# Keys, queries and values handed over with the dimensions in rows

## The chip, the core and the metric

The kernel runs on one core of a Trainium2 chip. Its time is device microseconds of the whole program. The engines named here: TensorE (PE; its weight loads are PEld), VectorE (DVE), ScalarE (ACT), GpSimd (POOL) and SyncE (SP), which issues nearly all transfers. Inputs lie in the chip's memory, and the form in which they lie there is chosen ahead of the launch, outside the time.

## The reference

```python
def _attn_ref(q, k, v):                     # B, H, S, D = 2, 8, 768, 64
    block, window = (32, 16)
    k_sum = k.reshape(B, H, nb, block, D).max(axis=3)
    v_sum = v.reshape(B, H, nb, block, D).mean(axis=3)
    scores_l = scale * np.matmul(q, k.transpose(0, 1, 3, 2))
    mask_l = np.abs(pos[:, None] - pos[None, :]) < window
    scores_s = scale * np.einsum('bhsd,bhnd->bhsn', q, k_sum) + np.log(block)
    scores_l_m = np.where(mask_l, scores_l, -1000000000.0)
    a = softmax of [scores_l_m, scores_s]   # written out in the reference
    return np.matmul(a, np.concatenate([v, v_sum], axis=2))

def _moe_ref(x, w_gate, w_val, w_out):      # 1536 tokens, 512 -> 1536 -> 512
    g = x @ w_gate
    return (g * sigmoid(g) * (x @ w_val)) @ w_out

def _moe2_ref(x, w_in, w_out):              # 512 -> 2048 -> 512
    h = x @ w_in
    return (h * np.clip(h + 3.0, 0.0, 6.0) / 6.0) @ w_out
```

Each query sees the 31 keys within 15 positions, and 24 summaries of blocks of 32 keys (the maximum of the keys, the mean of the values). The output goes through two MLPs. The weights are handed over in 8-byte floats.

## The kernel before, in words

**Tiles.** 1536 rows are cut into four token tiles of T = 384: t = 0, 1 are batch 0, t = 2, 3 batch 1. The 8 heads go in NP = 4 pairs c, whose 2 x 64 dimensions fill 128 partitions. A stage of attention is one t with its four pairs.

**Attention of one pair.** `keys` (once for each batch) loads k with the positions in rows, two parts of 384 positions, each by two transfers of 64 dimensions; TensorE turns each part by three transposes (`rows`, line 592), ScalarE or VectorE copies the bank into `kT[c]`, and VectorE takes the maxima over blocks into `ksum[c]` (line 621). `queries` does the same for 384 queries and multiplies by -1/8 on the way out. `values` (once for each batch) loads v with eight neighbouring positions in one of 96 partitions, adds halves three times on GpSimd or VectorE (line 636), and TensorE multiplies by a small matrix of 1/32 (line 642), which gives the 24 means; they are copied six times over into the first 24 rows of `vw[c]`. `load_vw` fills rows 24 to 119 of `vw[c]` with the 96 positions that each of six blocks of 64 queries can see. `scores` writes 120 columns for each of 384 queries (line 697); VectorE adds a mask and takes the top (717), ScalarE the exponentials (724), VectorE sums and reciprocals (736, 737), GpSimd or VectorE weighs (748), TensorE turns the weights (754), and `outputs` multiplies with `vw` (768). The result becomes x in two parts, a high and a rest (lines 273, 280).

**MLP.** Every product is three matmuls (lines 334 to 336): high by high, low by high, high by low. The weights come as 8-byte floats and are split on VectorE and ScalarE (lines 370 to 391, then 273 and 280), group by group; the first group is loaded and split while attention runs, the next ones behind it, into room that attention gives back.

**What sets the order.** `Plan` collects tasks with a rank, costs on each engine and what they read and write, schedules them once by those costs and emits the instructions of all engines in that order. Each engine then runs its list in order; semaphores make it wait. Transfers stand in SyncE's list too (those of pair 1 of t=0 in ScalarE's), so one that waits for its buffer holds back all behind it. Where TensorE's plan has a gap, `fill` puts up to ten matmuls on zeros there (line 835). Attention of t=1 to 3 is spread among the MLP's first group. The ranks are shifted by the table `LEAD`.

## Time and profile before

| what | us |
|---|---|
| median of 3 runs | 653.56 |
| lowest and highest | 653.07, 653.57 |
| profiled execution | 654.63 |
| its span, first to last instruction | 652.9 |
| TensorE busy | 640.2 (98%) |
| VectorE busy | 438.3 (67%) |
| ScalarE busy | 289.7 (44%) |
| GpSimd busy | 52.9 (8%) |

A busy share is a mean over the whole program: the first fifth, with attention in it, and the rest are two different programs. A matmul's time in the rows overlaps its neighbours', so what one costs is read from start to start. The idle time in brackets is that of the engine just before the row, with what ended it.

### The profile page before, as it was taken

Reading aid. Unit: us, or ns where it says so; the run is one execution under the profiler, and the core shown is the slowest. Engines: PE = TensorE matmul, PEld = TensorE weight load, DVE = VectorE, ACT = ScalarE, POOL = GpSimd, SP = SyncE. Lnnn points to the kernel's source line nnn. Section 1 sums busy time; section 2 is a strip of 40 time slices with the busy share of each in tenths; the row PEclk is TensorE's granted clock in tenths of the full one; section 3 lists DMA queues with packets and bytes.
Section 4 is the critical chain, followed back from the end, with each engine's and each line's share of the span. In section 5 each row is a group of like instructions: output and inputs, shape, how many; then the busy total and the mean of one; then the engine's idle time right before and its main releaser. Section 6 shows DMA issues by size and latency. Waiting matters only on the chain.

```text
span 652.9 us, 11688 instructions
## 1 busy us (share of the span) xinstructions
PE 640.2 (98%) x4576; PEld 601.1 (92%) x4576; DVE 438.3 (67%) x972; ACT 289.7 (44%) x674; POOL 52.9 (8%) x73
## 2 busy tenths in 40 slices
PE   7799999999999999999999999999999999999997
PEld 6688888999999999999999999999999999999996
DVE  3789974589997978369754997286738753333332
ACT  3788788455543433134322564354424332222220
POOL 3435443100000000000000000000000000000000
PEclk9989999999999999999999999999999999999999
DMA  8998944043433233003210133012301000000112
GB/s 185 220 225 232 193 85 140 1 130 132 159 130 98 97 97 97 1 27 103 81 50 0 66 103 124 1 65 64 131 1 40 25 1 0 2 1 0 50 49 96
DMA packets 73319, 53.84 MB, mean 82 GB/s; under 512 B 45744, under 2 KB 66736, under 8 KB 73264
## 3 DMA queue, kind: packets, MB, share of 16 engines
q1 hardware_dynamic: 70864, 52.51, 28.7%
q10 hardware_dynamic: 2400, 0.59, 0.6%
q8 instruction: 36, 0.59, 0.4%
q14 instruction: 19, 0.16, 0.1%
HBM read 49.94 MB, written 3.15 MB: 81 GB/s over the span
## 4 chain that ended last, share of the span: by engine, by line
PE 92%; DMA 4%; ACT 2%; issue 0%; SPq 0%; DVE 0%; POOL 0%; ACTq 0%; POOLq 0%
PE mm L334 16%; PE mm L335 15%; PE mm L336 15%; PE mmb L334 13%; PE mmb L335 13%; PE mmb L336 13%; PE at_s L697 2%; PE pv L768 2%; DMA vn<-in_v 2%; DMA early<-in_k 1%; PE at_t L754 1%; ACT p L724 1%; DMA kn<-in_k 1%; PE pv L835 1%; PE at_q L592 1%
## 5 line engine op out<-in xcount | busy, mean ns | idle before, releaser
L334 PE MATMUL mm<-x,wa 128*128 128x384 f32 x196 | 69.2, 353 | 0.0
L336 PE MATMUL mm<-x,wa 128*128 128x384 f32 x196 | 65.9, 336 | 0.0
L335 PE MATMUL mm<-x,wa 128*128 128x384 f32 x196 | 65.9, 336 | 0.0
L387 ACT ACTIVATE raw<-raw 128x512 f32<-128x512 f32 x68 | 46.2, 680 | 26.3 <-DVE bits L379 23.4
L335 PE MATMUL mmb<-x,wb 128*128 128x384 f32 x160 | 53.5, 335 | 0.0
L335 PE MATMUL mm<-x,wb 128*128 128x384 f32 x160 | 53.5, 335 | 0.0
L336 PE MATMUL mmb<-x,wb 128*128 128x384 f32 x160 | 53.5, 334 | 0.0
L336 PE MATMUL mm<-x,wb 128*128 128x384 f32 x160 | 53.5, 334 | 0.0
L334 PE MATMUL mm<-x,wb 128*128 128x384 f32 x160 | 53.5, 334 | 0.0
L334 PE MATMUL mmb<-x,wb 128*128 128x384 f32 x160 | 53.5, 334 | 0.0
L273 ACT ACTIVATE g<-u 128x384 fp32r<-128x384 f32 x61 | 32.0, 525 | 43.5 <-DVE u L431 22.6
L391 DVE SCALAR_TENSOR_TENSOR bits<-raw,bits 128x512 f32<-128x512 f32 x68 | 46.6, 685 | 1.1 <-ACT raw L387 0.6
L379 DVE SCALAR_TENSOR_TENSOR bits<-raw,bits 128x512 uint32<-128x512 uint32 x68 | 46.9, 690 | 0.4
L383 DVE SCALAR_TENSOR_TENSOR bits<-raw,bits 128x512 uint32<-128x512 uint32 x68 | 46.9, 690 | 0.1
L280 DVE TENSOR_TENSOR g<-u,g 128x384 fp32r<-128x384 f32 x59 | 33.5, 568 | 19.2 <-ACT g L273 19.1
L273 ACT ACTIVATE gb<-u 128x384 fp32r<-128x384 f32 x51 | 26.8, 525 | 37.4 <-DVE u L431 19.2
L724 ACT ACTIVATE p<-p,st 128x120 f32<-128x120 f32 x96 | 36.9, 388 | 10.5 <-DVE st L717 10.5
L335 PE MATMUL mmb<-x,wa 128*128 128x384 f32 x124 | 41.5, 335 | 0.0
L336 PE MATMUL mmb<-x,wa 128*128 128x384 f32 x124 | 41.5, 334 | 0.0
L334 PE MATMUL mmb<-x,wa 128*128 128x384 f32 x124 | 41.5, 334 | 0.0
L273 ACT ACTIVATE wb<-bits 128x512 fp32r<-128x512 f32 x33 | 20.9, 633 | 44.6 <-DVE bits L391 16.9
L280 DVE TENSOR_TENSOR gb<-u,gb 128x384 fp32r<-128x384 f32 x51 | 28.3, 555 | 16.7 <-ACT gb L273 16.6
(198 smaller groups left out, 1659.9 us busy)
## 6 DMA issues: line engine op xcount, KB each, us to landing
raw<-in_moe_w_out SPq DMA_DIRECT2D x28, 512.0 KB, 3.2
raw<-in_moe_w_in SPq DMA_DIRECT2D x16, 512.0 KB, 3.7
raw<-in_moe_w_gate SPq DMA_DIRECT2D x12, 512.0 KB, 4.2
raw<-in_moe_w_val SPq DMA_DIRECT2D x12, 512.0 KB, 3.6
vw<-in_v SPq DMA_DIRECT2D x32, 120.0 KB, 3.6
vn<-in_v SPq DMA_DIRECT2D x8, 384.0 KB, 4.6
out<-oacc SPq DMA_DIRECT2D x11, 256.0 KB, 2.0
kn<-in_k SPq DMA_DIRECT2D x16, 96.0 KB, 4.7
```

Source lines behind the costliest of these rows:

```text
L273: nc.scalar.activation(dst, src, AF.Copy, scale=scale)
L280: eng[e].tensor_tensor(dst, a, b, ALU.subtract)
L334: nc.tensor.matmul(ps, lhsT=lh, rhs=rh, start=j == 0, stop=False)
L335: nc.tensor.matmul(ps, lhsT=ll, rhs=rh, start=False, stop=False)
L336: nc.tensor.matmul(ps, lhsT=lh, rhs=rl, start=False, stop=j == n_k - 1)
L379: nc.vector.scalar_tensor_tensor(t, high_w(), 0xC0000000, t, ALU.bitwise_and, ALU.bitwise_or)
L383: nc.vector.scalar_tensor_tensor(t, low_w(), 29, t, ALU.logical_shift_right, ALU.bitwise_or)
L387: nc.scalar.activation(mag, mag, AF.Abs)
L391: nc.vector.scalar_tensor_tensor(as_f(), mag, 2.0**-15, as_f(), ALU.is_ge, ALU.mult)
L697: nc.tensor.matmul(tiles["at", "s", *names[h]][a * QB : (a + 1) * QB, j, cols], lhsT=q2[hs, u * QB : (u + 1) * QB], rhs=rhs, start=True, s ...
L724: nc.scalar.activation(a, a, AF.Exp, bias=s[:, 0, n : n + 1], scale=-1.0, accum_out=s[:, 1, n : n + 1])
L768: nc.tensor.matmul(tiles[pv][h * D : (h + 1) * D, u * QB : (u + 1) * QB], lhsT=vw[c][:NK, u, h * D : (h + 1) * D], rhs=tiles[pts[h]][:, u ...
```

## The change

The inputs q, k and v are handed over with the dimensions of a head pair in 128 rows and the positions along each row (k with 16 zeros at both ends), and v a second time, as `vu`, with the 64 positions of a block in rows, then the block, then the 128 dimensions, with a block of zeros at both ends. Weights of `w_gate`, `w_val` and `w_in` are handed over so that a partition's 4 KB lie in one piece (four pieces of 1 KB before). So:

- keys: one transfer for a pair, straight into `kT`; no turn, no copy, no memset of its ends. `kT` exists for each batch; three of batch 0 lie in the room of x of t=3.
- queries: one transfer, straight to where scores read them; the factor -1/8 moves into the mask instruction, whose table is scaled to it.
- values: VectorE sums the 768 columns of [128, 768] by blocks of 32 into [128, 24], TensorE transposes this, and the factor 1/32 is applied in the copy to `vw`.
- `vw`: three transfers still, now of 64, 16 and 16 partitions with 3 KB each; its memset is gone.
- costs of transfers in the plan's tasks are lowered to suit; `LEAD` and the other numbers of the plan stay.

```diff
+def laid_out(name, a):
+    if name in ("q", "k", "v"):
+        a = a.reshape(B, NP, 2, S, D).transpose(0, 1, 2, 4, 3).reshape(B, NP, P, S)
+        if name == "k":
+            a = np.pad(a, ((0, 0), (0, 0), (0, 0), (HALO, HALO)))
+    elif name == "vu":
+        a = a.reshape(B, NP, 2, S // QB, QB, D).transpose(0, 1, 4, 3, 2, 5).reshape(B, NP, QB, S // QB, P)
+        a = np.pad(a, ((0, 0), (0, 0), (0, 0), (1, 1), (0, 0)))
+    elif name in ("moe_w_gate", "moe_w_val", "moe2_w_in"):
+        a = a.reshape(KC, P, -1, P).transpose(2, 1, 0, 3)
...
     rings = dict(mm=4, mmb=4, at=3, pv=1, wa=9, wb=9, raw=3, bits=2, u=3, g=5, gb=5,
-                 kn=4, qn=2, v3=1, qT=2, p=4, st=2, pt=4)
+                 v3=1, qT=4, p=4, st=2, pt=4)
...
     def load_vw(t, c):
+        b, half = divmod(t, 2)
+        u0, to = half * NB, vw[c]
+        nc.sync.dma_start(out=to[NS + HALO : NS + HALO + QB], in_=vu[b, c, :, u0 + 1 : u0 + 1 + NB])
+        nc.sync.dma_start(out=to[NS : NS + HALO], in_=vu[b, c, QB - HALO :, u0 : u0 + NB])
+        nc.sync.dma_start(out=to[NS + HALO + QB :], in_=vu[b, c, :HALO, u0 + 2 : u0 + 2 + NB])
...
     def keys(rank, b, c):
+        n = ("kT", b, c)
+        def load():
+            second(2 * b, c).dma_start(out=kT[b, c], in_=k[b, c])
...
-            add(rank, {"pe": 0.3}, turn, r=[n, ("cs",)], w=[ps, ("kT", c)])
-            add(rank - LEAD["k_put"], {"act": 0.4, "dve": 0.47}, put, r=[ps], w=[("kT", c)])
...
-        add(rank, {"dve": 0.87}, most, r=[("kT", c)], w=[("ksum", c)])
+        add(rank - LEAD["k_load"], {"dma": 1.35}, load, w=[n])
+        add(rank, {"dve": 0.87}, most, r=[n], w=[("ksum", c)])
...
+        def total():
+            nc.vector.tensor_reduce(new(v3, [P, NS]), vn[b, c].rearrange("q (n i) -> q n i", i=BLOCK), AX.X, ALU.add)
+        def turn():
+            tiles[ps] = new_bank(ps, [NS, P])
+            nc.tensor.transpose(tiles[ps], tiles[v3], ident)
         def put(e):
-            copy(e, vw[c][:NS], tiles[ps].unsqueeze(1).to_broadcast([NS, NB, P]))
-        add(rank, {"pool": 1.23, "dve": 0.6}, halve(4), w=[room], port=True)
-        add(rank, {"pool": 0.72, "dve": 0.33}, halve(2), w=[room], port=True)
-        add(rank, {"pool": 0.45, "dve": 0.2}, halve(1), r=[room], w=[v3], port=True)
-        add(rank, {"pe": 0.33}, mean, r=[v3, ("masks",)], w=[ps, ("vs", c)])
+            copy(e, vw[c][:NS], tiles[ps].unsqueeze(1).to_broadcast([NS, NB, P]), 1.0 / BLOCK)
+        add(rank, {"dve": 0.87}, total, r=[room], w=[v3])
+        add(rank, {"pe": 0.12}, turn, r=[v3, ("cs",)], w=[ps, ("vs", c)])
...
     def queries(rank, t, c):
-        add(rank, {"pe": 0.3}, turn, r=[n, ("cs",)], w=[ps, qt])
-        add(rank - LEAD["q_put"], {"act": 0.4, "dve": 0.47}, put, r=[ps], w=[qt])
+            second(t, c).dma_start(out=tiles[n], in_=q[b, c, :, half * T : (half + 1) * T])
+        add(rank - LEAD["q_load"], {"dma": 0.68}, load, w=[n])
...
-                scale=1.0, scalar=3.0e38, op0=ALU.add, op1=ALU.min, accum_out=tiles[st][:, 0, h * TR + r : h * TR + r + 1],
+                scale=-SCALE, scalar=3.0e38, op0=ALU.add, op1=ALU.min, accum_out=tiles[st][:, 0, h * TR + r : h * TR + r + 1],
```

The plan is made anew, so the order of all engines moves a little. Three places show it; numbers in the names are t, c and part.

TensorE in stage t=2, around the means of values of pair 0 of batch 1 (`at_v_1_0`), before: `at_q` and `at_k` are turns of queries and keys, `mm_8` an MLP product of x of t=1.

```order
L592 MATMUL at_q_2_1_1301<-cs_89,qn_2_1_1183 128x128 x3
L334 MATMUL mm_8_1310<-x1_1017,wa_0_0_1_0_724 128x384
L335 MATMUL mm_8_1310<-x1_1017,wa_0_0_1_0_724 128x384
L336 MATMUL mm_8_1310<-x1_1017,wa_0_0_1_0_724 128x384
L592 MATMUL at_k_1_2_0_1318<-cs_89,kn_1_2_0_1224 128x128 x3
L642 MATMUL at_v_1_0_1323<-v3_1_0_1273,cs_89 24x128
```

And now:

```order
L351 MATMUL mm_9_1199<-x1_878,wa_0_0_0_1_715 128x384
L352 MATMUL mm_9_1199<-x1_878,wa_0_0_0_1_715 128x384
L353 MATMUL mm_9_1199<-x1_878,wa_0_0_0_1_715 128x384
L351 MATMUL mm_10_1238<-x1_878,wa_0_0_1_1_807 128x384
L352 MATMUL mm_10_1238<-x1_878,wa_0_0_1_1_807 128x384
L353 MATMUL mm_10_1238<-x1_878,wa_0_0_1_1_807 128x384
L615 MATMUL at_v_1_0_1248<-cs_89,v3_1_0_1231 24x128
```

The turns of keys and queries are gone from between the MLP's matmuls, and the product by the matrix of 1/32 is a transpose.

VectorE at the start of the program, before; `vn` are the loaded values, `at_s` the scores, `ksum` the maxima.

```order
L621 TENSOR_REDUCE ksum0_98<-kT0_90 128x24
L636 TENSOR_TENSOR vn0_0_167<-vn0_0_167 96x2x256
L636 TENSOR_TENSOR vn0_1_254<-vn0_1_254 96x2x256
L717 ISA p_0_0_0_226,st_0_0_225<-at_s_0_0_0_218,cs_89 128x120
L717 ISA st_0_0_225 128x1
```

And now; `v3` are the sums of values.

```order
L598 TENSOR_REDUCE ksum0_94<-early_k_98 128x24
L611 TENSOR_REDUCE v3_0_0_198<-vn0_0_152 128x24
L598 TENSOR_REDUCE ksum1_95<-early_k_98 128x24
L611 TENSOR_REDUCE v3_0_1_220<-vn0_1_188 128x24
L676 ISA p_0_0_0_169,st_0_0_168<-at_s_0_0_0_157,cs_89 128x120
L676 ISA st_0_0_168 128x1
```

The sums and the maxima of pairs 0 and 1 now all stand ahead of the first mask add (`p<-at_s,cs`).

SyncE's list at the start, up to the first block of MLP weights (`raw`), before.

```order
L809 DMA cs_89<-in_cst 128x128
L554 DMA early3_107<-in_k 128x3x64 x4
L554 DMA early2_164<-in_q 128x3x64 x2
L575 DMA vn0_0_167<-in_v 96x2x512
L575 DMA vn0_1_254<-in_v 96x2x512
L812 DMA cs_89<-in_cst 128x384
L554 DMA early3_107<-in_k 128x3x64 x4
L554 DMA early2_164<-in_q 128x3x64 x2
L584 DMA vw0_94<-in_v 80x2x64
L588 DMA vw0_94<-in_v 96x5x64 x2
L575 DMA vn0_2_320<-in_v 96x2x512
L554 DMA early3_107<-in_k 128x3x64 x4
```

And now.

```order
L581 DMA vn0_0_152<-in_v 128x768
L581 DMA vn0_1_188<-in_v 128x768
L771 DMA cs_89<-in_cst 128x360
L595 DMA early_k_98<-in_k 128x800
L633 DMA early_q_99<-in_q 128x384
L586 DMA vw0_90<-in_vu 64x768
L587 DMA vw0_90<-in_vu 16x768
L588 DMA vw0_90<-in_vu 16x768
L581 DMA vn0_2_235<-in_v 128x768
L595 DMA kT0_3_100<-in_k 128x800
L633 DMA early_q_99<-in_q 128x384
L586 DMA vw1_91<-in_vu 64x768
```

What stood in four transfers of keys and two of queries stands in one each; the first block of weights comes behind 17 transfers where 29 stood before it.

## Rows read from the trace of the kernel before

**Rows 1.** The page, 40 slices of 16.3 us; each digit a slice, in tenths.
```profile
PE   7799999999999999999999999999999999999997
...
PEclk9989999999999999999999999999999999999999
...
DMA  8998944043433233003210133012301000000112
```

**Rows 2.** Windows: stretch, us, busy us and instructions of each engine, clock, DMA share, GB/s.
```profile
8.40:46.20 37.80, 30.67 (x543) 24.91 (x540) 29.55 (x106) 27.71 (x94) 15.54 (x18) 0.95 1.05 220
...
46.20:67.30 21.10, 20.84 (x314) 18.31 (x316) 19.85 (x69) 18.63 (x64) 10.11 (x12) 1.00 0.88 221
...
10.00:30.00 20.00, 15.96 (x329) 12.62 (x329) 13.69 (x56) 14.61 (x52) 8.28 (x12) 1.00 1.04 212
...
140.00:170.00 30.00, 30.00 (x175) 30.00 (x174) 29.60 (x57) 16.98 (x33) 0.00 (x0) 1.00 0.43 140
...
33.50:37.00 3.50, 3.50 (x24) 2.84 (x20) 3.36 (x8) 3.28 (x8) 1.81 (x2) 0.51 1.18 284
...
66.10:652.90 586.80, 582.48 (x3684) 551.46 (x3680) 389.52 (x801) 241.69 (x517) 24.90 (x29) 1.00 0.22 68
```

**Rows 3.** Timeline of TensorE: start us, us, line, operation, tiles, count, idle before.
```profile
15.39 0.52 PE L592 MATMUL mm_q<-cs,early 128*128 128x128 f32 x3 [1.46 <-DMA early<-in_q]
...
29.52 0.54 PE L754 MATMUL at_t<-cs,p 128*120 128x128 f32 x3 [1.12 <-POOL p L748]
...
31.14 0.34 PE L835 MATMUL at_t<-zeros 128*128 128x128 bf16 x3 [1.08 <-DVE st L717]
...
35.89 0.67 PE L334 MATMUL mm<-x,wa 128*128 128x384 f32 x1
...
60.38 0.49 PE L592 MATMUL at_k<-cs,kn 128*128 128x128 f32 x3
...
60.71 0.49 PE L592 MATMUL at_q<-cs,qn 128*128 128x128 f32 x3
...
65.27 0.92 PE L768 MATMUL pv<-pt,vw 120*64 120x64 f32 x24
...
71.23 0.40 PE L642 MATMUL at_v<-v,cs 96*24 96x128 f32 x2
...
71.56 0.44 PE L334 MATMUL mm<-x,wa 128*128 128x384 f32 x1
...
85.57 0.31 PE L697 MATMUL at_s<-ksum,qT 64*64 64x24 f32 x8
...
86.58 0.44 PE L334 MATMUL mm<-x,wa 128*128 128x384 f32 x1
...
89.88 0.42 PE L334 MATMUL mm<-g,wa 128*128 128x384 f32 x1
```

**Rows 4.** Timeline of VectorE, the same columns.
```profile
8.37 0.95 DVE L621 TENSOR_REDUCE ksum<-kT 128x24 f32<-128x768 f32 x1 [8.37 <-ACT kT L273]
...
18.27 0.28 DVE L717 CUSTOM_DVE_ANT_0 p<-at_s,cs 128x120 f32<-128x120 f32 x1 [2.46 <-PE at_s L697]
```

**Rows 5.** DMA, 0 to 125 us: packets by size; issues, KB each, us to landing.
```profile
DMA packets 51446, 20.88 MB, mean 167 GB/s; under 512 B 44640, under 2 KB 49504, under 8 KB 51424
...
early<-in_k SPq DMA_DIRECT2D x12, 96.0 KB, 3.9
```

**Rows 6.** Timeline of the DMA queue of SyncE: start us, us, line, tiles, count.
```profile
1.18 2.01 SPq L554 DMA_DIRECT2D early<-in_k  x4
...
21.82 0.55 SPq L370 DMA_DIRECT2D raw<-in_moe_w_gate  x1
```

**Rows 7.** Lines of VectorE, 0 to 125 us: busy us, mean ns, idle before.
```profile
L621 DVE TENSOR_REDUCE ksum<-kT 128x24 f32<-128x768 f32 x8 | 7.6, 946 | 8.4 <-ACT kT L273 8.4
...
L636 DVE TENSOR_TENSOR vn<-vn 96x512 f32<-96x512 f32 x5 | 3.9, 803 | 0.5 <-DMA vn<-in_v 0.5
...
L277 DVE COPY kT<-mm_k 128x384 f32<-128x384 f32 x2 | 1.1, 556 | 0.5 <-PE mm_k L592 0.5
```

More of the change, by code (lines that the diff above doesn't have):

```diff
@@ L33 @@
 N1, N2 = F1 // G1, F2 // G2
-WP = 96
 NEG = 1.0e9
+SCALE = 1.0 / D**0.5
 LEAD = dict(
@@ L543, in out2 @@
             add(rank, {"dma": 0.73 * n / DM}, store, r=[("o", t, m)])
-    kT = [ap_.tile([P, S + 2 * HALO], F32, name=f"kT{c}") for c in range(NP)]
-    vw = [ap_.tile([P, NB, P], F32, name=f"vw{c}") for c in range(NP)]
+    vw = [ap_.tile([NK, NB, P], F32, name=f"vw{c}") for c in range(NP)]
     ksum = [ap_.tile([P, NS], F32, name=f"ksum{c}") for c in range(NP)]
     vn = {}
-    def load_rows(dst, src, queue=nc.sync):
-        for h in range(2):
-            queue.dma_start(out=dst[:, :, h * D : (h + 1) * D], in_=src[h].rearrange("(r p) d -> p r d", p=P))
-    early = {}
-    def stage(kind, c, part):
-        x = 3 if kind == "k" else 2
-        if x not in early:
-            early[x] = xpool.tile([P, 8, TR, P], F32, tag=f"x{x}", name=f"early{x}")
-        return early[x][:, 2 * c + part]
+    early_k = xpool.tile([P, NP - 1, S + 2 * HALO], F32, tag="x3", name="early_k")
+    early_q = xpool.tile([P, 2, NP, T], F32, tag="x2", name="early_q")
+    kT = {(b, c): ap_.tile([P, S + 2 * HALO], F32, name=f"kT{b}_{c}") if b or c == NP - 1 else early_k[:, c]
+          for b in range(B) for c in range(NP)}
     def second(t, c):
@@ L573, in load_v @@
         room = xpool.tile([P, KC * T], F32, tag=f"acc{v_room(b, c)}", name=f"vn{b}_{c}")
-        vn[b, c] = room[:WP, : 16 * D].rearrange("p (h r d) -> p h r d", h=2, r=8)
-        nc.sync.dma_start(out=vn[b, c], in_=v[b, 2 * c : 2 * c + 2].rearrange("h (p r) d -> p h r d", r=8))
+        vn[b, c] = room[:, :S]
+        nc.sync.dma_start(out=vn[b, c], in_=v[b, c])
     def load_vw(t, c):
-        b, s0 = divmod(t * T, S)
-        va = v[b, 2 * c]
-        end, cut0, cut1 = (0, HALO, NW) if s0 == 0 else (NB - 1, 0, QB + HALO)
@@ L581, in load_vw @@
-        inner = 1 if s0 == 0 else 0
-        first = s0 + end * QB - HALO + cut0
-        src = bass.AP(va.tensor, va.offset + first * D, [[D, cut1 - cut0], [S * D, 2], [1, D]])
-        nc.sync.dma_start(out=vw[c][NS + cut0 : NS + cut1, end, :].rearrange("p (h d) -> p h d", h=2), in_=src)
-        for h in range(2):
-            first = h * S + s0 + inner * QB - HALO
-            src = bass.AP(va.tensor, va.offset + first * D, [[D, NW], [QB * D, NB - 1], [1, D]])
-            nc.sync.dma_start(out=vw[c][NS : NS + NW, inner : inner + NB - 1, h * D : (h + 1) * D], in_=src)
@@ L590, in rows @@
-    def rows(ps, src):
-        for r in range(TR):
-            nc.tensor.transpose(ps[:, r, :], src[:, r, :], ident)
-    def keys(rank, b, c):
-        for part in range(2):
-            n = ("kn" if b else "k0", b, c, part)
-            def load(n=n, part=part):
-                if b == 0:
-                    tiles[n] = stage("k", c, part)
-                else:
-                    new(n, [P, TR, P])
-                load_rows(tiles[n], k[b, 2 * c : 2 * c + 2, part * T : (part + 1) * T], second(b, c))
-            add(rank - LEAD["k_load"], {"dma": 1.05}, load, w=[n])
-            ps = prep_bank(b, "k", b, c, part)
-            def turn(n=n, ps=ps):
-                tiles[ps] = new_bank(ps, [P, TR, P])
-                rows(tiles[ps], tiles[n])
-            def put(e, part=part, ps=ps):
-                dst = kT[c][:, HALO + part * T : HALO + (part + 1) * T].rearrange("q (r p) -> q r p", p=P)
-                copy(e, dst, tiles[ps])
-            add(rank, {"pe": 0.3}, turn, r=[n, ("cs",)], w=[ps, ("kT", c)])
-            add(rank - LEAD["k_put"], {"act": 0.4, "dve": 0.47}, put, r=[ps], w=[("kT", c)])
+        b, half = divmod(t, 2)
@@ L655, in queries @@
-        b, s0 = divmod(t * T, S)
+        n = ("qT" if t > 1 else "q0", t, c)
+        b, half = divmod(t, 2)
         def load():
             if t < 2:
-                tiles[n] = stage("q", c, t)
+                tiles[n] = early_q[:, t, c]
             else:
-                new(n, [P, TR, P])
-            load_rows(tiles[n], q[b, 2 * c : 2 * c + 2, s0 : s0 + T], second(t, c))
-        add(rank - LEAD["q_load"], {"dma": 1.05}, load, w=[n])
-        def turn():
-            tiles[ps] = new_bank(ps, [P, TR, P])
-            new(qt, [P, TR, P])
-            rows(tiles[ps], tiles[n])
@@ L671, in put @@
-        def put(e):
-            copy(e, tiles[qt], tiles[ps], -1.0 / float(D) ** 0.5)
-        add(rank, {"pe": 0.3}, turn, r=[n, ("cs",)], w=[ps, qt])
-        add(rank - LEAD["q_put"], {"act": 0.4, "dve": 0.47}, put, r=[ps], w=[qt])
+                new(n, [P, T])
+            second(t, c).dma_start(out=tiles[n], in_=q[b, c, :, half * T : (half + 1) * T])
+        add(rank - LEAD["q_load"], {"dma": 0.68}, load, w=[n])
     def scores(rank, t, c):
-        half, qt = t % 2, ("qT", t, c)
+        b, half, qt = t // 2, t % 2, ("qT" if t > 1 else "q0", t, c)
```

53 lines of the change are left out of this document (16 added, 37 removed).

## The prediction

> **What bounds the kernel now.** I read the page's 40 slices first [rows 1]: the reader is to see that TensorE stands at 9 tenths from the third slice on, that its clock sits a little under full in that third slice, and that the DMA row is nearly full only over the first five slices, some 80 us. So there are two regimes, and the change touches only the first. Next the windows [rows 2]: from 66.1 us to the end TensorE is busy 582.48 of 586.8 us, and in 140 to 170 us it is busy all 30 us. Whatever is late after 66 us is late because TensorE has that much to do. Before that it has room: in 8.4 to 46.2 us it is busy 30.67 of 37.80, and part of this is matmuls on zeros. The third view is the timeline of TensorE [rows 3]: the first MLP matmul starts at 35.89 us, and the last output of pair 3 of stage t=1 (the matmuls on vw) starts at 65.27 and takes 0.92, so it ends near 66.1. I call that end T, 66.1 us. The sum has two terms: where T lies, and what TensorE still has to do behind it.
>
> VectorE is the helper that decides T. In 46.2 to 67.3 us it is busy 19.85 of 21.10 (94%) [rows 2]; in the stage before it 29.55 of 37.80, with waits for scores such as 2.46 us ahead of the first mask add of pair 1 [rows 4], scores that in turn stood behind 1.46 us of waiting for that pair's queries [rows 3]. In 10 to 30 us the DMA share is 1.04 at 212 GB/s; in 140 to 170 us a share of 0.43 gives 140, which is 326 GB/s at full share [rows 2]. The packets say why: 44640 of 51446 in the first 125 us are under 512 B [rows 5].
>
> **Term 1, TensorE's work behind T.** A turn of three transposes of keys or queries costs 0.33 us from its start to the next start (60.38 to 60.71) [rows 3]. Behind T the order of before has 5 such turns of keys and 7 of queries; all go: 12 x 0.33 = 4.0 us. The four means of values of batch 1 cost 0.33 each (71.23 to 71.56) and become one transpose, for which I take a third of a turn, 0.11: 4 x 0.22 = 0.9 us. Bounds: 0 (as dear as the mean) and 0.33 (free) each; it is nearest to the turn's row, being the same operation. Two moves run against each other: the order puts the scores of t=2 pair 0 ahead of T, 1.0 us (85.57 to 86.58) [rows 3], and puts 21 MLP matmuls behind T that were ahead of it, at 30 us / 175 = 0.171 each [rows 2], 3.6 us. So 586.8 - 4.0 - 0.9 - 1.0 + 3.6 = 584.5 us.
>
> **Term 2, where T lies.** Stage t=0 first, until the last x of t=0 (46.2 us). VectorE starts there at 8.37 with the maxima of keys [rows 4]. Ahead of them stood four transfers of keys, the first issued at 1.18 [rows 6], two turns and two copies; now it is one transfer on SP, issued at the same place, and the chain of turn and copy is gone. A transfer of 96 KB of early keys takes 3.9 us to land at the median [rows 5]. One four times as large lands between that and 3.9 + 1.4 us (288 KB more at 212 GB/s), so VectorE starts between 5.1 and 6.5. The pieces are long, and the keys and queries of pair 1 now stand at the head of ScalarE's queue and come at the same time; I take 5.5.
>
> Its work in this stage: out go 4 copies of 0.556 and 4 halvings of 0.803, 5.4 us; in come 4 sums of columns, priced by the maxima of keys, the same reduction over the same 128x768, at 0.946 [rows 7], 3.8 us, and one copy of weights, 0.5; the order moves about 2 us of mask adds, reciprocals and weight splitting to the next stage. 29.55 - 5.4 + 3.8 + 0.5 - 2.0 = 26.4 us.
>
> The Trainium skill (VectorE: DVE Perf Modes, "The perf-mode tier table" and "Rules for kernel authors") speaks against this step: a reduction runs only in the slowest mode, and where it lies on the hot path another form is advised. The row agrees: 0.946 us against 0.803 for a halving [rows 7]. By that rule alone VectorE, the busiest helper, gains nothing from the change, which is the second rival below.
>
> Then VectorE's idle time in the stage, 37.80 - 29.55 = 8.25 us [rows 2]. It was waiting for keys and queries that passed through DMA, TensorE and a copy. Twelve turns and their copies go from in front of the scores and transfers come in longer pieces, but the masks still stand behind five transfers on SP, the sums of values of pairs 0 and 1 now stand ahead of the first mask add and wait for their transfers, and ScalarE's exponentials still alternate with VectorE. Bounds 0 and 8.25; I take half, 4.1. The stage ends at 5.5 + 26.4 + 4.1 = 36.0 us.
>
> Stage t=1: VectorE had 19.85 us of work, loses one halving and one copy (1.3), gains one pair of maxima (0.9) and the 2 us moved here: 21.4 us. At the 94% of before that is 22.8, and T lies 1.2 us ahead of its end as before (67.3 less 66.1): 36.0 + 22.8 - 1.2 = 57.6 us. TensorE alone would not be later: its 30 us between 35.89 and T lose 7 turns and 21 matmuls, 2.3 + 3.6, and leave some 24 us of work, of which the first part can run from about 30 us: the first weight block, issued at 21.82 us before, stands behind 17 transfers on SP where 29 stood, at 2.01 / 4 = 0.5 us for issuing one [rows 6], so 6 us earlier. 30 + 24 = 54 us is ahead of 57.6.
>
> What else the change touches, and costs nothing here: ScalarE loses more copies than VectorE and is not ahead of it; the longer pieces of weights come where TensorE has no idle time; GpSimd's halvings and memsets go, and its weighing of exponentials stays. The factor of the scores and the 1/32 of the means ride in instructions that stood there before. Two w_out blocks now stand on SP behind vw loads that wait for outputs of t=1 pairs 0 and 1. Those outputs come before T, and the blocks are first used by matmuls of g on wa, at 89.88 us before [rows 3], some 24 us behind T; that work of TensorE hides the landing and the splitting. Without it the price would be the landing of a transfer, 4 to 6 us.
>
> The Trainium skill (SBUF — State Buffer, "Door 1: The DMA port swizzle") says that a transfer to few partitions reaches few ports. The halos of vw are now two transfers of 16 partitions for each pair and stage, 49 KB each; by its four ports of about 27 GB/s an estimate is 0.45 us each, where the 326 GB/s of the late weights would take 0.15. The eight of t=0 would cost 2.4 us more of DMA time if nothing ran beside them, and by that the prediction would be 645. No row of before shows such a transfer, and the sum doesn't use it.
>
> **Sum.** 57.6 + 584.5 = 642.1 us of span, against 652.9. The profiled execution took 654.63, so 1.7 lies around the span: 643.8, which is 10.8 below it, 1.65%. On the median of 653.56 that is 642.8; I predict 643 us. Its own range is 639 to 647 (idle time of 0 to 8.25 in the first stage).
>
> **Rivals.**
> 1. The forecast: both terms. For it: TensorE is full behind T, so work removed there counts at once. 0.58.
> 2. VectorE takes the gain of the start. Its work to T hardly changes (49.4 before, 47.8 now: the sums take back most of what copies and halvings give). If all its idle time of 8.25 stays and one more wait like the 2.46 of before comes ahead of the first mask add, which now stands behind two sums of values, T = 57.6 + 4.1 + 2.5 = 64.2 and the time is 649.4. For it: 94% busy. Against it: the waits shown there are for turned keys and queries. 0.20.
> 3. TensorE alone bounds from the first MLP matmul on: start at 35.89 less the 6 us of SP and the 2.9 of VectorE's start, 27; 24 us of work; T = 51, 636 us. For it: the order has only 14 fills behind the first MLP matmul. Against it: VectorE would have to do 47.8 us from 5.5 to 52 without a pause. 0.13.
> 4. Slower, by the clock of TensorE. In 33.5 to 37 us the granted clock was 0.51, the 1.2 GHz level, and ahead of it TensorE had waited 1.12 and 1.08 us at 29.5 and 31.1 [rows 2, 3]. The change takes the turns out of a stage in which TensorE is already thin. If the half clock held from the first MLP matmul, 24 us of work would take 48 and T would be 27 + 48 = 75, some 660 us. For the time to pass 653.56 T must pass 69, 42 us for 24 us of work, so it decides from some 36 us of half clock on, ten times what the rows show; in 10 to 30 us, at 15.96 of 20 busy, the clock held, and the order keeps 122 of 132 fills. 0.05.
> 5. No difference: T stays, and the 2.3 us that term 1 takes off are lost to new waits behind T; about 653. 0.04.
>
> Chances, with 0.2% (1.3 us) as what a measurement of this kernel can tell from no change: faster 0.92, same 0.03, slower 0.05. The range goes from rival 3 to rival 2: 635 to 650 us.
>
> **What would show it.** In the profile after, no line of the transposes of keys and queries, and a TensorE timeline with the first MLP matmul near 30 us and the last output of t=1 ending near 57.6; from there to the end about 584.5 us, nearly all busy. VectorE's window of t=0 holds about 26 us of work with about 4 us idle; the first maximum of keys starts near 5.5 us. The DMA share of the first 30 us falls, or its GB/s rises well over 212. The prediction is wrong if T stays past 62 us (term 2, VectorE or masks), if TensorE is idle for more than 2 us behind T (term 1), or if the granted clock is half for more than some 5 us.

## The result, and the profile after

| what | before | after |
|---|---|---|
| median, us | 653.52 (4 runs, 653.07 to 653.57) | 644.89 (4 runs, 642.36 to 647.07) |
| profiled execution, us | 654.63 | 642.36 |
| its span, us | 652.9 | 640.4 |
| T, end of the last output of stage t=1, us | 66.1 | 56.45 |
| span behind T, us | 586.8 | 583.95 |

The ratio of after to before is 0.9868 (95%: 0.9827 to 0.9909): 8.6 us faster, against 643 predicted. The profiled execution is the fastest of the four. They spread by 4.7 us, where those of before spread by 0.5; in the order of their times the mean granted clock of TensorE was 1.000, 0.997, 0.992 and 0.991. I come back to that: the profile of before lay at 0.996 and has a stretch at half clock [rows 2], so the 12.5 us between the two spans is not all the change's.

The page after: TensorE, its granted clock, the DMA engines (40 slices of 16 us) and the DMA's packets. They answer to [rows 1, 5].

```profile
PE   7798999999999999999999999999999999999997
...
PEclk9999999999999999999999999999999999999999
...
DMA  9886440244331321014200233031201000000112
...
DMA packets 18918, 54.07 MB, mean 84 GB/s; under 512 B 2609, under 2 KB 5169, under 8 KB 18865
```

The DMA is now nearly full (8 or 9 tenths) over three slices instead of five, and nothing of the clock is missing in the third slice. Short packets are nearly gone: 2609 in the whole program, where the first 125 us of before had 44640.

The windows after, with the columns of [rows 2]: both stages of attention (5.89 is VectorE's first instruction, 35.81 and 57.59 the ends of the last x of t=0 and t=1), 10 to 30 us as before, then the two regimes on either side of T.

```profile
5.89:35.81 29.92, 23.26 (x499) 18.62 (x498) 26.52 (x97) 22.61 (x81) 6.85 (x8) 1.00 0.91 282
...
35.81:57.59 21.78, 18.77 (x315) 16.32 (x314) 21.04 (x81) 18.78 (x68) 7.90 (x9) 1.00 0.87 287
...
10.00:30.00 20.00, 15.82 (x331) 12.31 (x331) 17.48 (x76) 16.51 (x62) 6.85 (x8) 1.00 0.94 281
...
5.89:56.45 50.56, 40.88 (x806) 33.80 (x804) 46.42 (x175) 40.30 (x144) 14.75 (x17) 1.00 0.89 284
...
56.45:640.40 583.95, 580.45 (x3613) 550.68 (x3613) 386.29 (x791) 238.31 (x504) 25.47 (x25) 1.00 0.20 66
```

Read the third number group, VectorE: 26.52 us of work in 29.92 (89%), then 21.04 in 21.78 (97%). It was 29.55 in 37.80 and 19.85 in 21.10. In 10 to 30 us its work rose from 13.69 to 17.48 us: it is fed. The DMA moves 281 GB/s at a share of 0.94 there, 299 at full share; before it was 212 at 1.04, 204 at full share. Behind T TensorE is idle for 3.5 us in 584 (583.95 less 580.45).

The timeline of TensorE after: the first MLP matmul, two waits, the last output of t=1 [rows 3].

```profile
27.25 0.45 PE L351 MATMUL mm<-x,wa 128*128 128x384 f32 x1
...
30.54 0.45 PE L353 MATMUL mm<-x,wa 128*128 128x384 f32 x1 [1.27 <-DVE x L297]
...
32.38 0.72 PE L786 MATMUL at_s<-zeros 128*128 128x128 bf16 x10 [0.74 <-ACT pt L290]
...
55.53 0.92 PE L727 MATMUL pv<-pt,vw 120*64 120x64 f32 x24
```

VectorE's first two pieces of work [rows 4]: the maxima of keys, and a sum of values.

```profile
5.89 0.95 DVE L598 TENSOR_REDUCE ksum<-early_k 128x24 f32<-128x768 f32 x1 [5.89 <-DMA early_k<-in_k]
7.49 0.95 DVE L611 TENSOR_REDUCE v<-vn 128x24 f32<-128x768 f32 x1 [0.65 <-DMA vn<-in_v]
```

Both wait for a transfer and for nothing else; before, the first waited for a copy of turned keys.

### The profile page after: what moved, and what is told of

It is laid out like the page before. It is cut to its first block, busy times and chain, and to the rows that moved or that the text cites. A ratio compares the mean times of both kernels' runs of the same rounds, so it can differ in the third digit from the quotient of the medians.

```text
span 640.4 us, 11332 instructions
## 1 busy us (share of the span) xinstructions
PE 626.2 (98%) x4462; PEld 589.4 (92%) x4462; DVE 432.7 (68%) x963; ACT 279.9 (44%) x649; POOL 40.6 (6%) x47
## 2 busy tenths in 40 slices
DMA packets 18918, 54.07 MB, mean 84 GB/s; under 512 B 2609, under 2 KB 5169, under 8 KB 18865
## 3 DMA queue, kind: packets, MB, share of 16 engines
HBM read 50.19 MB, written 3.15 MB: 83 GB/s over the span
## 4 chain that ended last, share of the span: by engine, by line
PE 93%; DVE 3%; ACT 2%; DMA 1%; issue 1%; POOL 0%; SPq 0%; POOLq 0%
PE mm L351 16%; PE mm L352 16%; PE mm L353 16%; PE mmb L353 13%; PE mmb L351 13%; PE mmb L352 13%; PE at_s L656 2%; PE pv L727 2%; PE at_t L713 1%; DVE p L676 1%; ACT p L683 1%; DMA vn<-in_v 1%; ACT pt L290 0%; DVE x L297 0%; DVE v L611 0%
```

## The experiments

For each kernel I split its profile at T, and T by VectorE: when it starts, what it works to T, how long it is idle in between. Every number is from windows like those above; idle is the length less the work. The twelve runs were made on four occasions, and the kernel before ran beside them each time, at medians of 654.7 to 655.0; the ratios compare with those.

| kernel | ratio to before (95%) | median | VectorE starts | works | idle | T | behind T |
|---|---|---|---|---|---|---|---|
| before | 1 | 653.5 to 655.0 | 8.37 | 48.84 | 8.98 | 66.19 | 586.71 |
| after, again | 0.9827 (0.9800 to 0.9854) | 644.64 | 5.73 | 46.49 | 4.17 | 56.39 | 584.0 |
| weights alone | 0.9990 (0.9974 to 1.0007) | 653.54 | 7.32 | 48.64 | 9.86 | 65.82 | 586.18 |
| short pieces, no turns | 0.9987 (0.9969 to 1.0004) | 653.24 | 7.41 | 46.81 | 10.05 | 64.27 | 586.43 |
| keys, queries short, no turns | 0.9921 (0.9894 to 0.9947) | 649.95 | 7.21 | 46.45 | 6.64 | 60.30 | 589.70 |
| long pieces, all turns | 0.9983 (0.9965 to 1.0001) | 653.38 | 7.06 | 48.33 | 10.86 | 66.25 | 586.15 |
| the same, pair 1 issued first | 0.9929 (0.9907 to 0.9952) | 650.01 | 7.82 | 48.48 | 4.66 | 60.96 | 586.24 |
| idle turns behind T | 0.9904 (0.9876 to 0.9931) | 649.10 | 5.84 | 47.22 | 6.49 | 59.55 | 588.75 |
| idle turns ahead of T | 0.9867 (0.9846 to 0.9889) | 645.62 | 5.70 | 46.52 | 7.30 | 59.52 | 583.98 |
| sums of values twice | 0.9853 (0.9829 to 0.9876) | 645.51 | 5.77 | 49.99 | 3.75 | 59.51 | 583.99 |
| halvings for sums | 0.9883 (0.9861 to 0.9904) | 646.92 | 6.07 | 47.67 | 7.83 | 61.57 | 584.13 |
| more zeros in gaps | 0.9865 (0.9836 to 0.9894) | 647.41 | 5.86 | 47.27 | 6.36 | 59.49 | 585.91 |
| new order | 0.9800 (0.9772 to 0.9827) | 641.63 | 5.92 | 45.25 | 3.67 | 54.84 | 585.36 |

The split holds up: in the changed kernel, in its second run, with sums twice and with turns ahead of T, the last column is 583.95 to 584.0, whatever T is. T of before is 66.19 here by its row (65.27 + 0.92), and this is its window to T:

```profile
8.37:66.19 57.82, 50.44 (x825) 42.42 (x826) 48.84 (x172) 45.70 (x154) 24.62 (x28) 0.97 0.98 221
```

**The changed kernel again.** No edit.

> The changed kernel once more, unaltered. Its four runs so far lie at 642.36, 643.65, 646.14 and 647.07 us, with a mean granted clock of 1.000, 0.997, 0.992 and 0.991. Theory C: the spread is the clock of TensorE; a run is as long as the clock is low, about 0.5 us for each 0.001 of mean clock, median near 645. Theory D: the spread has another source (transfers that land at other times); then time and clock are not in one order, and runs at 1.000 reach 646.

Five executions: 642.30 and 642.29 at a granted clock of 1.000, 644.64 and 644.80 at 0.995, 646.03 at 0.992. The four of the first table fall in line. So the 4.7 us of spread go with TensorE's clock; below I compare at equal clock where it matters.

**Turns behind T.** TensorE's twelve turns are put back behind T, on the identity, with nothing that waits for them.

```diff
         def weighted():
             tiles[pv] = pv_bank[:, :T]
...
+            for _ in range(3 * (1 + (c + 1) % 2) if t > 1 else 0):
+                nc.tensor.transpose(spare, ident, ident)
```

> The changed kernel with twelve idle turns (36 transposes of the identity into the spare part of the output bank) added to TensorE's list behind T, in the output tasks of t=2 and t=3; nothing else moves. Theory A (TensorE is full behind T, work there counts at once): 12 x 0.33 = 4.0 us more than the changed kernel at the same clock, 646.4 at full clock. Rival (some slack behind T takes it up): under 1 us more.

At a granted clock of 1.000 it took 646.26, against 642.30: 3.96 us, for 12 x 0.33 = 4.0. At 0.997 it is 3.9, at 0.995 4.5, at 0.992 4.1 to 4.2, from one execution of this run each. The first term's main part is confirmed within some tenths of a microsecond. (The median differs by 4.5, with other clocks mixed in.)

**Sums twice.** VectorE gets 4 x 0.95 us more work ahead of T.

```diff
-            nc.vector.tensor_reduce(new(v3, [P, NS]), ...)
+            for _ in range(2 if b == 0 else 1):
+                nc.vector.tensor_reduce(new(v3, [P, NS]), ...)
```

> The changed kernel with each of the four sums of values of batch 0 done twice on VectorE, 4 x 0.87 us more work in stage t=0, the same order. Theory A (VectorE decides T): the first mask add starts 1.8 us later, T lies 2 to 3.5 us later than 56.4, and the time is 2 to 3.5 us more at the same clock. Rival (TensorE alone bounds from the first MLP matmul on, or the 3.4 us of idle time of VectorE in that stage take it up): under 0.7 us more.

At 0.997 it took 645.5, the changed kernel 643.65: 1.9 us; at 0.995 646.23 against 644.7: 1.5. In the profile T moved by 3.06 us for 3.57 us more work, but 3.4 us of that stage ran at the lower clock. VectorE's work is on the path, but about half of it is taken up by waits that were there anyway: less than my theory, more than the rival.

**Turns ahead of T.** Twenty idle turns before the scores of t=0 and t=1.

```diff
         def go(j):
...
+            for _ in range(3 * (3 - t) if j == 0 and t < 2 else 0):
+                nc.tensor.transpose(spare, ident, ident)
```

> The changed kernel with twenty idle turns of three 128x128 transposes put before the scores of stages t=0 (three for each pair) and t=1 (two for each pair): TensorE's work of the turns, 20 x 0.33 = 6.6 us, without their copies and transfers. Theory V (VectorE and its waits set T, TensorE has some 6 us of room before T): T moves by 0 to 2.5 us, the time by as much. Rival 3 of the prediction (TensorE alone decides from the first MLP matmul on): T moves by 4 to 6.6 us. If idle turns keep the clock up in the stage, the spread of the five times shrinks as well.

T moved by 3.1 us and the time by 3.15 at 1.000 (645.45 twice and 645.62 once, against 642.30), for 6.6 us of TensorE's work: between the theory's 0 to 2.5 and rival 3's 4 to 6.6. VectorE's work stayed and its idle time rose by 3.2. So neither engine alone sets T: scores go to VectorE, x comes back to TensorE, and work put on either side counts by about half. All five runs lay at 0.997 or 1.000, where the changed kernel's went down to 0.991; the expectation named that as a sign that idle turns keep the clock up, though five runs are few.

**Halvings for sums.** The values as in the kernel before, all else as after.

```diff
...
-        add(rank, {"dve": 0.87}, total, r=[room], w=[v3])
-        add(rank, {"pe": 0.12}, turn, r=[v3, ("cs",)], w=[ps, ("vs", c)])
+        add(rank, {"pool": 1.23, "dve": 0.6}, halve(4), w=[room], port=True)
+        add(rank, {"pool": 0.72, "dve": 0.33}, halve(2), w=[room], port=True)
+        add(rank, {"pool": 0.45, "dve": 0.2}, halve(1), r=[room], w=[v3], port=True)
+        add(rank, {"pe": 0.33}, mean, r=[v3, ("masks",)], w=[ps, ("vs", c)])
```

> The changed kernel, but the values as in the kernel before: rows of tokens in, three halvings by GpSimd or VectorE and a matmul with 1/32, for one sum of columns by VectorE and a transpose. Terms of the prediction: four means behind T cost 0.9 us more than four transposes; VectorE gets back what GpSimd takes of the halvings and gives 0.95 for each pair. Theory B (the sums are a wash): within 1.5 us of the changed kernel at the same granted clock. Rival D (a reduction is VectorE's slowest form, and VectorE sets T): 1.5 to 3 us faster, T 2 to 4 us earlier. Rival H (GpSimd's long chain of halvings is late for the values): 1.5 to 4 us slower.

At 0.992 it took 646.44, 646.55 and 649.53, where the changed kernel took 646.03 and 646.14; by the medians it is 2.0 to 2.3 us slower. It is not faster, which rules out rival D; at the same clock the two lie within a microsecond, but for the one of 649.53. The timelines show why rival H has something: TensorE stands still for GpSimd's chain (here the mean of values of pair 0).

```profile
10.91 0.62 PE L624 MATMUL mm_v<-v,cs 96*24 96x128 f32 x2 [2.09 <-POOL v L618]
```

Between "a wash" and "halvings cost 1.5 to 4 us" the runs don't decide: the clock of the stage was low as well (0.68 over 8 to 24 us).

**Weights alone.** Of the change only the weights' layout, in the kernel before.

```diff
...
-            return w[:, f * P : (f + 1) * P].bitcast(U32).rearrange("(c p) f -> p c f", p=P)
+            return w[f].bitcast(U32).rearrange("p c f -> p (c f)")
...
```

> The kernel before, with one part of the change alone: the weights of gate, val and w_in handed over so that a 128x128x4 block is 4 KB in a row of a partition, instead of eight pieces of 512 B. Theory A (the gain is the turns gone behind T and the earlier T; the weights come where TensorE has no idle time): within 1.3 us of the kernel before, and the first MLP matmul within 1 us of 35.9. Rival W (the short pieces of weights held up the shared DMA in the first 60 us): some 2 to 6 us faster than before, with T of 60 to 64 us.

The ratio's interval includes 1 and T moved by 0.4: no gain. (The pieces before were four of 1 KB, not eight of 512 B as I wrote; the number of packets under 512 B is the same, 45744.)

**Short pieces, no turns.** The changed kernel, but the inputs lie so that a row comes in pieces of 320 B (keys) and 256 B (queries, `vu`).

```diff
...
-            second(2 * b, c).dma_start(out=kT[b, c], in_=k[b, c])
+            second(2 * b, c).dma_start(out=kT[b, c].rearrange("p (n w) -> p n w", w=80), in_=k[b, c].rearrange("n p w -> p n w"))
...
-            second(t, c).dma_start(out=tiles[n], in_=q[b, c, :, half * T : (half + 1) * T])
+            second(t, c).dma_start(
+                out=tiles[n].rearrange("p (n w) -> p n w", w=64),
+                in_=q[b, c, half * T // 64 : (half + 1) * T // 64].rearrange("n p w -> p n w"))
...
```

> The changed kernel with no turns and the sums by columns, but keys in pieces of 320 B, queries and the values beside them in pieces of 256 B, as short as those of the kernel before. Theory P (the transfers set the start: 212 GB/s in short pieces against 281 in long ones): the first maximum of keys comes 1 to 2 us later than 5.9, T 3 to 6 us later than 56.5, and the time some 3 to 5 us longer than the changed kernel at the same granted clock. Rival C (what went at the start is the chain of turn and copy): T within 1.5 us of 56.5 and the time within 1.5 us.

The whole gain is gone: 653.24, ratio 0.9987. That is more than theory P said. T and what lies behind it, in the windows of this kernel, with 8 to 16 and 56 to 64.27 us beside them:

```profile
7.41:64.27 56.86, 45.51 (x800) 38.04 (x800) 46.81 (x175) 40.78 (x144) 14.72 (x17) 0.86 1.10 241
64.27:650.70 586.43, 581.44 (x3613) 551.37 (x3613) 385.55 (x788) 238.34 (x504) 25.34 (x25) 1.00 0.21 66
8.00:16.00 8.00, 7.30 (x131) 6.22 (x131) 6.08 (x25) 3.76 (x16) 0.00 (x0) 0.58 1.19 262
56.00:64.27 8.27, 5.28 (x58) 3.85 (x58) 7.99 (x23) 4.94 (x14) 1.79 (x2) 0.68 1.08 205
```

At an equal clock of 0.995 it took 651.91 and 653.61 against 644.64 and 644.80, so most of the loss is not the clock of single executions. Three things add up in the profile: the transfers come late (VectorE starts 1.5 us later and is idle 5.9 us longer), the clock is lower while TensorE waits (0.86 over the stage), and 2.5 us more are spent behind T. The Trainium skill (DMA: Bandwidth & Descriptors, "Specifications") asks for pieces of at least 512 B for the full rate; the trace agrees, with 241 GB/s at a share of 1.10 (219 at full share) against 284 at 0.89 (319) to T.

**Keys and queries short, `vu` long.** The same edit without its part on `vu`.

> The changed kernel with keys in pieces of 320 B and queries in pieces of 256 B, while the values beside the queries stay in pieces of 3 KB. With all three short the time was 653.2 and T 64.3. Theory K (keys and queries are what VectorE and the scores wait for, and their short pieces hold the queue): more than half of the loss stays, T 60 to 64, the time 4 to 8 us above the changed kernel. Rival U (the values beside the queries, as many bytes as all queries and half the keys together, fill the engines of the DMA and delay all behind them): less than a third stays, T below 59, the time less than 3 us above the changed kernel.

The time is 5.3 us above the changed kernel by the medians, T 60.30: theory K, with some three fifths of the loss. Part of that is clock: at equal clock it is 2.0 to 4.8 us. In the profiled execution, the slowest of the six, 9.6 us of span above that of after, 3.9 lie ahead of T (at a granted clock of 0.94 to T) and 5.75 behind it, in a wait that neither theory named: VectorE waits for weights of `w_out`, which stand in SyncE's list behind keys and queries of batch 1, and TensorE then waits, at turns of weighed exponentials.

```profile
65.97 0.43 DVE L391 TENSOR_SCALAR bits<-raw 128x512 uint32<-128x512 uint32 x1 [4.52 <-DMA raw<-in_moe_w_out]
```
```profile
74.00 0.54 PE L718 MATMUL at_t<-cs,p 128*120 128x128 f32 x3 [3.94 <-POOL p L712]
```

**Long pieces, all turns.** The opposite corner: the kernel before with its own order, turns and copies; keys and queries in pieces of 1.5 KB, `vu` and weights as after.

```diff
...
-        for h in range(2):
-            queue.dma_start(out=dst[:, :, h * D : (h + 1) * D], in_=src[h].rearrange("(r p) d -> p r d", p=P))
+        queue.dma_start(out=dst, in_=src.rearrange("p r h d -> p r (h d)"))
...
```

> The kernel before with all its turns, copies, halvings and its order on the engines, but keys, queries, the values beside the queries and the weights handed over so that a row of a partition is one long piece (1.5, 1.5, 3 and 4 KB in place of 256 and 512 B). It is the opposite corner to the kernel with short pieces and no turns, whose T (end of the last output of stage t=1) came at 64.3 us with VectorE starting at 7.4 and idle for 10.1 us to T, against 5.9 and 4.1 in the changed kernel. Theory P (the pieces decide T): VectorE starts 1 to 1.5 us earlier than 8.4, its idle time to T falls from 9.0 to some 5, T comes at 60 to 62 us, and the time falls by 4 to 6 us against the kernel before; the work of turns behind T stays, so it does not reach the changed kernel. Rival C (only pieces and turns together move T, since the chain turn, copy, scores waits as long): T within 1.5 us of 66 and the time within 1.5 us of the kernel before.

Nothing is won: 653.38, T 66.25, though the DMA's share to T falls from 0.98 to 0.75:

```profile
7.06:66.25 59.19, 51.98 (x828) 43.28 (x827) 48.33 (x172) 45.49 (x154) 24.84 (x28) 0.94 0.75 226
```
Theory P falls in this form. The Trainium skill (DMA: Bandwidth & Descriptors, "Rules for kernel authors") advises to coalesce many small transfers; the trace agrees as far as the DMA's share goes, but the time of this kernel did not follow. The timelines say what holds T instead. First ScalarE and the transfers that stand in its list (ACTq):

```profile
5.76 0.49 ACT L287 ACTIVATE kT<-mm_k 128x384 f32<-128x384 f32 x1 [3.75 <-PE mm_k L597]
5.77 0.38 ACTq L565 DMA_DIRECT2D early<-in_k  x1
6.54 0.49 ACT L287 ACTIVATE kT<-mm_k 128x384 f32<-128x384 f32 x1 [0.29 <-PE mm_k L597]
7.64 0.33 ACTq L565 DMA_DIRECT2D early<-in_k  x1
8.02 0.49 ACT L287 ACTIVATE qT<-mm_q 128x384 f32<-128x384 f32 x1 [0.99 <-DMA vn<-in_v]
9.32 0.33 ACTq L565 DMA_DIRECT2D early<-in_q  x1
```

The transfers of pair 1 stand between the copies of pair 0. The first is issued when the first copy begins, and that one waits for turned keys. Then TensorE and VectorE of the same kernel:

```profile
13.17 0.52 PE L597 MATMUL mm_k<-cs,early 128*128 128x128 f32 x3 [2.39 <-DMA early<-in_k]
```
```profile
20.84 0.28 DVE L722 CUSTOM_DVE_ANT_0 p<-at_s,cs 128x120 f32<-128x120 f32 x1 [4.19 <-PE at_s L702]
```

Keys of pair 1 arrive at 13.2, its scores at 20.8. In the changed kernel there is no copy ahead of them:

```profile
0.74 0.40 ACTq L595 DMA_DIRECT2D early_k<-in_k  x1
1.17 0.45 ACTq L633 DMA_DIRECT2D early_q<-in_q  x1
```

**The same, pair 1 issued first.** Only these three instructions move, to the head of ScalarE's list; the order on all other engines is the same.

```diff
...
         order, pe = self.schedule(best_rank), None
+        order.sort(key=lambda t: not t.head)
...
-            add(rank - LEAD["k_load"], {"dma": 1.05}, load, w=[n])
+            add(rank - LEAD["k_load"], {"dma": 1.05}, load, w=[n]).head = (b, c) == (0, 1)
...
-        add(rank - LEAD["q_load"], {"dma": 1.05}, load, w=[n])
+        add(rank - LEAD["q_load"], {"dma": 1.05}, load, w=[n]).head = (t, c) == (0, 1)
```

> The kernel before with long pieces, as in the run that kept all turns and gained nothing (653.4 us, T at 66.25), with three instructions moved: the transfers of keys and queries of pair 1 are issued at the head of ScalarE's queue. In that run they stood there between copies of turned keys and queries of pair 0 and were issued at 5.77, 7.64 and 9.32 us, so that TensorE waited 2.39 us for the keys of pair 1 until 13.2 and VectorE 2.50 and 4.19 us up to 20.8; in the changed kernel, whose queue has no such copies, they go out at 0.74 and 1.17. Everything else of the order is the same on all engines. Theory Q (that place in the queue held the start): the three are issued by 2 us, TensorE turns the keys of pair 1 by 9 us, VectorE's idle time to T falls from 10.9 to 5 to 7, T comes at 60 to 63 us and the time falls to 647 to 650. Rival R (turns and copies of pair 0, 2 and 3 are as late a chain of their own): T stays within 1.5 us of 66 and the time within 1.5 us of 653.4; then the turns and copies themselves are what holds the start.

650.01, ratio 0.9929: an interval that does not meet that of the run without the move. T is 60.96, VectorE's idle time 4.66 instead of 10.86, though VectorE starts 0.76 us later. The issue rows, VectorE's first wait for scores of pair 1, and the two windows:

```profile
0.73 0.89 ACTq L567 DMA_DIRECT2D early<-in_k  x2
1.65 0.45 ACTq L567 DMA_DIRECT2D early<-in_q  x1
```
```profile
15.70 0.28 DVE L724 CUSTOM_DVE_ANT_0 p<-at_s,cs 128x120 f32<-128x120 f32 x1 [0.96 <-PE at_s L704]
```
```profile
7.82:60.96 53.14, 49.28 (x827) 41.57 (x828) 48.48 (x172) 45.16 (x154) 24.79 (x28) 1.00 0.82 238
60.96:647.20 586.24, 582.37 (x3681) 551.39 (x3680) 389.12 (x801) 242.01 (x517) 25.11 (x29) 1.00 0.20 67
```

Theory Q: three instructions, with all turns and copies still there, are worth some 5 us of T in the profiles, and 0.54% or 3.5 us by the ratios (part of both is clock: in the profiles 0.94 to T in the run without the move, 1.00 here). At equal clock the move is worth less: at 1.000 648.93 to 651.09 (four executions) against 651.64 and 651.84, at 0.997 650.14 and 650.96 against 652.26 to 653.47, some 2 us by the means. The two ran on different occasions.

**More zeros in gaps.** A remedy for the falling clock: up to 40 matmuls on zeros in a gap of TensorE's plan instead of 10.

```diff
-FILL_MAX = 10
+FILL_MAX = 40
```

> The changed kernel with up to 40 instead of 10 matmuls on zeros in a planned gap of TensorE, 213 instead of 122 or so. Theory C: more activity ahead of the MLP keeps the clock up, all runs at 0.998 or more and within 1 us of 642.5, so 2 us below the median of the unaltered kernel. Rival: the clock falls as before, as the pauses at 28.9, 31.6, 50 and 53 us are not foreseen by the plan and hold no fill; same spread, and up to 1 us more from fills that overrun their gap.

It took 647.41, 2.8 us more than the changed kernel, and its granted clocks were 0.991 to 0.997; at equal clock it is 0.3 to 1.2 us above. Its profile has two stretches at the lower level, and two waits ahead of the first:

```profile
32.90:36.30 3.40, 3.40 (x62) 2.98 (x62) 2.50 (x6) 2.03 (x7) 0.00 (x0) 0.50 0.77 250
...
56.80:63.60 6.80, 6.60 (x39) 6.04 (x40) 5.62 (x15) 3.08 (x11) 0.00 (x0) 0.50 0.84 274
```
```profile
30.93 0.44 PE L353 MATMUL mm<-x,wa 128*128 128x384 f32 x1 [1.28 <-DVE x L297]
...
32.78 1.34 PE L786 MATMUL at_s<-zeros 128*128 128x128 bf16 x12 [0.76 <-ACT pt L290]
```

The theory behind it falls. The plan puts zeros where it sees a gap, and the waits that the chip has are elsewhere: ahead of 32.90 TensorE had waited 1.28 us at 30.93 and 0.76 at 32.78, as the changed kernel does at 30.54 and 32.38.

**A new order.** The same instructions as after, with ranks and leads of the plan fitted to them (the change had kept those of before).

```diff
...
-LAG = 2.58
-MASKS = -3.54
-PAIR_GAP = 4.06
-MAIN = 28.05
+LAG = 3.65
+MASKS = -3.99
+PAIR_GAP = 6.23
+MAIN = 27.04
...
-SPAN = 12.44
-NEXT, NEXT_END = -3.40, 23.95
+SPAN = 13.18
+NEXT, NEXT_END = -2.59, 21.03
...
```

> The changed kernel with the same instructions but another set of ranks and leads for the planner, fitted to the new instructions (the changed kernel kept those of the kernel before): the turns of exponentials and their weighing stand later, the copies of the sums earlier, and 66 MLP matmuls stand ahead of T where 51 stood. Theory V (VectorE's work and idle time set T, TensorE is full behind it): the 15 matmuls at 0.171 us are 2.6 us less behind T, and T moves by -2 to +1; the time falls by 1.5 to 4.5 us, to 638 to 641 at the full granted clock. Rival O (the order was good enough, and waits on the chip fall otherwise than the planner thinks): within 1.3 us of the changed kernel or slower.

641.63, ratio 0.9800, faster than both kernels at equal clock: 640.6 and 640.9 at 1.000 (642.3 after), 641.6 and 641.9 at 0.997 (643.65), 643.82 at 0.992 (646.1). At equal clock that is 1.4 to 2.3 us, at the lower end of what was expected; the intervals of the two ratios overlap. T is 54.84, VectorE works 1.2 us less ahead of it. The other half of theory V, 2.6 us less behind T, did not come: the time behind T is 1.4 us longer. TensorE works 0.9 us less there but is idle for 5.85 us instead of 3.5, of which one wait, with no cause that the profile shows, is 1.26. Its two windows, and that wait:

```profile
5.92:54.84 48.92, 43.00 (x807) 36.64 (x804) 45.25 (x165) 39.51 (x139) 16.14 (x19) 0.97 0.89 283
54.84:640.20 585.36, 579.51 (x3614) 548.06 (x3614) 377.12 (x778) 237.50 (x511) 43.14 (x43) 1.00 0.20 66
```
```profile
63.22 0.31 PE L656 MATMUL at_s<-ksum,qT 64*64 64x24 f32 x8 [1.26 <-issue]
```

## Why the prediction came out

**Term 1, TensorE's work behind T: 584.5 predicted, 583.95 measured.** The turns are worth what the row said (3.96 against 4.0, by the run with idle turns). The smaller parts were not taken apart; together they are 0.55 off. One sign that I had named against this term did come: TensorE idle for more than 2 us behind T. It is 3.5 us. The sign was badly set: by my own row the kernel before, which I called full there, was idle for 4.3 (586.80 less 582.48).

**Term 2, T: 57.6 predicted, 56.45 measured.** VectorE's start 5.5, measured 5.89; the first keys went out at 1.18, as said (the list of SyncE shown for the new order begins only behind its first three transfers). The end of t=0 36.0, measured 35.81: work 26.4, measured 26.52; idle 4.1, measured 3.40. Stage t=1 22.8 at 94%, measured 21.78 at 97%; T 1.2 ahead of its end, measured 1.14. The first MLP matmul came at 27.25, where I had said about 30: the first block of weights was issued at 12.58 us where 21.82 stood, 9 us earlier and not 6 (SPq is SyncE's list). With short pieces and the same list it went out at 19.14: SyncE's list moves on as the transfers ahead do.

```profile
12.58 0.42 SPq L385 DMA_DIRECT2D raw<-in_moe_w_gate  x1
```

**The number.** Predicted was a gain of 10.8 us. The first table has 8.6, the second occasion 10.4 by the medians. At a clock of 1.000, before took 652.05 to 653.79 (seven executions, median 652.76) and after 642.29 to 642.36 (three), 10.5 us apart. In the profile at 1.000 the two terms are 0.55 and 1.15 us too high; the first median, in which slower clocks take part, lies 1.9 above the forecast. The forecast had no term for the clock, and that the two errors partly cancel is luck.

**The step that was only half understood is the idle time.** I halved 8.25 us for want of a row, and named three reasons without prices: turns and copies that go, longer pieces, masks. That the size came out near (3.40 against 4.1) was luck; the reasons were incomplete. Removing the turns with pieces left short gives VectorE nothing back (idle 10.05 to T), long pieces with the turns left neither (10.86). What the prediction said of pair 1, that its transfers now stand at the head of ScalarE's list, was used only for the start. It is the piece that was missing: with long pieces and that place alone, idle time falls to 4.66. So the gain of T is no sum of parts that each give some: late issue of pair 1, with long pieces and all turns, left T at 66.25, and short pieces, with the turns gone and pair 1 at the head, at 64.27 (there with a granted clock of 0.86 to T, whose share of the loss was not taken apart). The place in the list alone, with the short pieces of before, was not run.

The windows to T say where the rest came from, both at a clock of 1.00. From the run with the place to the changed kernel T falls by 4.51 us: VectorE starts 1.93 earlier (7.82 to 5.89), works 2.06 less (48.48 to 46.42) and is idle 0.52 less (4.66 to 4.14). So the place gives back the idle time, and the rest of the change (turns and copies gone, sums for halvings, the order made anew, not taken apart) gives the start and the work.

By the ratios, of the 1.73% of the changed kernel run again (11.3 us), 0.17% come with long pieces (an interval that includes nothing), 0.54% with the place in the list, and the remaining 1.02% (6.7 us) when turns and copies go and the order is made anew: 2.3 us of it behind T (586.24 to 583.95), 4.5 ahead of it in the profiles. The earlier comparison has 1.32% in all; the split's last share is as uncertain as that. At a clock of 1.000 the same steps are some 1.0, 2 and 7.4 us of 10.5.

**Rival 2, VectorE takes the gain.** Not seen: T is far below 64.2, and the halvings in place of the sums are not faster. The Trainium skill (VectorE: DVE Perf Modes, "Rules for kernel authors") calls a reduction the slowest form and advises to restructure. The rows here do not show that it is slower: a reduction takes 0.95 us for 768 columns, a halving 0.80 for 512. And restructuring it into halvings won nothing in this kernel.

**Rival 3, TensorE alone.** It would have had T at 51. The run with turns ahead of T says it is half right: 6.6 us of TensorE's work moved T by 3.1. The new order, with T at 54.84, goes part of that way.

**Rival 4, the clock.** It did not turn the sign, but the mechanism is there. The profiled execution shows no fall; others of the same kernel do, by their mean clock, and the most they lost is 4.8 us. An estimate from the run with more zeros, whose profile at a mean of 0.991 has 3.4 and 6.8 us at the lower level: the execution of the changed kernel at 0.991 had about 10 us of it, more than the 5 us that I had named as a sign. Before had such a stretch at 33.5 us in its profile, and its runs on later occasions spread as widely, 652.1 to 657.2, so this is not a cost that the change brought. Rival 5 is out.

Not settled: what tips the clock. The same waits at 30 and 32 us were followed by a fall in the run with more zeros and by none in the profiled run after. And the halos of 16 partitions: no run takes them apart from the rest; by the rule of the Trainium skill (SBUF — State Buffer, "Door 1: The DMA port swizzle") the forecast would have been 645, and the trace does not decide: to 60 us, transfers of 16 partitions (48 KB) land in 5.2 us at the median, those of 64 partitions (192 KB) in 5.8, and neither ran alone.

## What to carry to other kernels

Look in which engine's list a transfer is issued and what stands ahead of it there: a transfer that needs nothing may wait for a copy that needs everything. When two causes hold the same start, undo each alone and both together before you credit either; alone, each looked worth nothing here. Compare at equal granted clock, too: it took more than a third off the gain of one step. And split the time at the point where the bounding engine becomes full: what is removed behind it counts in full, what is removed ahead of it counts by how far it moves that point.
